# A DiT attention block with adaptive layer norm: V before Q and K, from the scale alone, and the shift's share of V added after P V

## The chip, the core and the metric

The kernel runs on one core of one Trainium2 chip. The metric is device time in microseconds (us) of one execution; lower is better. Five engines work side by side, each in the order of its own queue: TensorE (PE, with its weight loads PEld), VectorE (DVE), ScalarE (ACT), GpSimd (POOL) and SyncE (SP), which here only issues DMA transfers. PE writes to PSUM alone, which has eight banks; the other engines work on SBUF and PSUM (POOL here on SBUF alone).

## The reference

B = 2 samples of N = 256 tokens, D = 1152, all inputs bfloat16. `w_mod` is 1152 x 6912, `wqkv` 1152 x 3456, `wo` 1152 x 1152.

```python
mod = (_silu(c) @ w_mod).reshape(B, 6, 1, D)
shift_a, scale_a, gate_a, shift_m, scale_m, gate_m = [mod[:, i] for i in range(6)]
h = _layernorm(x, axis=-1) * (1 + scale_a) + shift_a
qkv = h @ wqkv
q, k, v = (qkv[..., :D].copy(), qkv[..., D:2 * D].copy(), qkv[..., 2 * D:].copy())
p = _softmax(jnp.einsum('bqd,bkd->bqk', q, k) * D ** (-0.5), axis=-1)
a = jnp.einsum('bqk,bkd->bqd', p, v) @ wo
return x + gate_a * a
```

Only the first three of the six parts of `mod` are used. The rows of `p` sum to 1, so a term of `v` that is the same for every token of a sample, such as `shift_a @ wv`, comes out of `p @ v` unchanged.

## The kernel before

The 512 tokens are four tiles of 128 (`TT`); the 1152 features are nine groups of 128 (`KT`). Everything fits in SBUF: 19.8 MB are read once.

*Start.* `c` and x tiles 0 and 2 come on SP's queue, x tiles 1 and 3 on ACT's. PE transposes `c`, then runs 13 matmuls of no use (`junk_ps`). `silu(c)` is laid out 96 times side by side (`scT_rep`, L173), so that the small products for scale and shift have 96 and 56 columns instead of 2. DVE makes the statistics and normalised tiles (`xn`) of tokens 0 to 2, ACT those of tile 3; the reciprocal root is made on POOL for tiles 0 to 2. PE transposes `xn` and DVE and ACT copy it to `xnT` (features on partitions).

*Scale.* `scale_block(kk)`: nine matmuls for each of nine row blocks `wm` of `w_mod`, which arrive in nine transfers (L146). A first matmul with a row of ones puts the 1 of 1 + scale into PSUM. Then DVE makes `hTs = xnT * (1 + scale)`, 18 pieces of 128x256.

*First five features of Q.* They are begun from `hTs`, before the shift is known: `qkv_step(k)` (L302) adds feature group k to five banks `accs`; the weights `wA` come in three transfers. Among these steps stand the shift's matmuls (`shift_block`, L309; `H_AFTER_K` says after which step). When the shift is there, its share of the five features is made by 45 matmuls of 2 columns (`bias_ps`, L329) and added when the banks are emptied to `qkT`; 18 pieces `hT = xnT * (1 + scale) + shift` are made on DVE (12) and ACT (6).

*The other 13 features of Q and K* are made from `hT`, one bank each, and copied by ACT (L383). Then the scores S (`s_ps`, L414), then V, twelve groups of 128x384 (`v_group`, L429), under which softmax runs on DVE and ACT. Then P is transposed, then P V for both samples (L485), copied to `attnT` two feature groups at a time, then the output projection with gate and residual, tile by tile (L498). The last 384 columns of the last tile use weights already multiplied by the gate (`wo_last`, nine products on POOL, L483).

*Gate.* `gacc` (L397): DVE multiplies nine row blocks of `w_mod`'s third part with `silu(c)` and adds them, for each sample; `partition_all_reduce` on POOL (L409) sums over partitions and broadcasts. The second all-reduce is tied behind the softmax by a dependency (L464).

*Order.* Part of each of PE's, DVE's and ACT's order is pinned by hand (`pe_seq`, `dve_seq`, `act_seq`, L533); the rest is set by the scheduler. PSUM is 5 banks `mm` and 3 `pre`. SP issues the weights in the order in which they are used; an issue waits until the eighth transfer before it has landed.

Of the kernel before, what the change touches and what calls it, by code (L numbers as in the profile page):

```python
# [16 lines left out]
def kernel(  # L17
# [8 lines left out]
):  # L26
    nc = tc.nc
    P = 128
    B, N, D = x.shape
    T = B * N  # L30
    KT = D // P
    TT = T // P
# [5 lines left out]

    NACC = 5
    WA = NACC * P  # L40
    KSPLIT = 4
    NRS = 96
    NRH = 56
    KH = (KT + 1) // 2
    H_AFTER_K = [4, 4, 4, 5, 5, 6, 6, 6, 6]
    N_JUNK = 13
# [4 lines left out]
    wmod_v = w_mod.rearrange("(kk p) (s n) -> p kk s n", p=P, s=6)  # L51

# [5 lines left out]
    psum = ctx.enter_context(tc.tile_pool(name="psum", bufs=5, space=PSUM))  # L58
    psum_pre = ctx.enter_context(tc.tile_pool(name="psum_pre", bufs=3, space=PSUM))

    SCHED = mybir.DependencyInfo(mybir.DependencyClass.NoSync, mybir.DependencyReason.SCHED_ONLY)
    pe_seq = []
    dve_seq = []
    act_seq = []

    class _Rec:

        def __init__(self, eng, seq):
            self._eng, self._seq = eng, seq
# [12 lines left out]
    vec = _Rec(nc.vector, dve_seq)  # L82
    sca = _Rec(nc.scalar, act_seq)
    ten = _Rec(nc.tensor, pe_seq)

    def pin(seq):
        names, insts = set(), []
        for r in seq:
            if r.ins.name not in names:
                names.add(r.ins.name)  # L90
                insts.append(r)
        for a, b in zip(insts, insts[1:]):
            tc.add_manual_dep(b.ins, a.ins.name, SCHED, reason="pinned engine order")

    ident = const.tile([P, P], BF16)
    nc.gpsimd.memset(ident, 0.0)
    nc.gpsimd.affine_select(
# [3 lines left out]
    ones_bf = const.tile([P, P], BF16)  # L101
    nc.gpsimd.memset(ones_bf, 1.0)
    ones_row = const.tile([1, 512], BF16)
    nc.gpsimd.memset(ones_row, 1.0)
    junk_rhs = const.tile([P, 512], BF16)
    nc.gpsimd.memset(junk_rhs, 1.0)
    eps_t = const.tile([P, 1], F32)
    nc.gpsimd.memset(eps_t, EPS)
    neg_half = const.tile([P, 1], F32)
    nc.gpsimd.memset(neg_half, -0.5)  # L110

    c_sb = const.tile([2 * KT, P], BF16)
    x_sb = act.tile([P, TT, D], BF16)
    nc.scalar.preload_act_table_set("natural_log_exp_and_others")
    nc.sync.dma_start(out=c_sb, in_=c.rearrange("b (k p) -> (b k) p", p=P))  # L115
    for t in range(TT):
        eng = nc.sync if t % 2 == 0 else nc.scalar
        eng.dma_start(out=x_sb[:, t, :], in_=x_f[t * P : (t + 1) * P, :])

    wA = wpool.tile([P, KT, WA], BF16)  # L120
    rest_chunks = [(WA, 2 * P), (WA + 2 * P, 3 * P)]
    c0 = WA + 5 * P
    while c0 < 2 * D:
        w_ = min(CW, 2 * D - c0)
        rest_chunks.append((c0, w_))
        c0 += w_
    for vc in range(NCH):
        rest_chunks.append((2 * D + vc * CW, CW))
    wq_rest = []
    for i, (c0, w_) in enumerate(rest_chunks):  # L130
        wq_t = wpool.tile([P, KT, w_], BF16, tag=f"wq_rest{i}")
        wq_rest.append(wq_t)

    def w_cols(col, width):
        if col + width <= WA:
            return wA, col
        for (c0, w_), t_ in zip(rest_chunks, wq_rest):
            if c0 <= col and col + width <= c0 + w_:
                return t_, col - c0
        raise AssertionError((col, width))  # L140

    wmpool = ctx.enter_context(tc.tile_pool(name="wmpool", bufs=1))
    wmS, wmH = [], []
    for kk in range(KT):
        wm = wmpool.tile([P, D], BF16, tag=f"wS{kk}")
        nc.sync.dma_start(out=wm, in_=wmod_v[:, kk, 1, :])  # L146
        wmS.append(wm)
    nc.sync.dma_start(out=wA[:, 0:1, :], in_=wqkv_v[:, 0:1, 0:WA])
    nc.sync.dma_start(out=wA[:, 1:KSPLIT, :], in_=wqkv_v[:, 1:KSPLIT, 0:WA])
    nc.sync.dma_start(out=wA[:, KSPLIT:, :], in_=wqkv_v[:, KSPLIT:, 0:WA])  # L150
    for kk in range(KT):
        wm = wmpool.tile([P, D], BF16, tag=f"wH{kk}")
        nc.sync.dma_start(out=wm, in_=wmod_v[:, kk, 0, :])
        wmH.append(wm)

    cT_ps = psum_pre.tile([P, 2 * KT], BF16, tag="pre")
    pe_seq.append(ten.transpose(cT_ps, c_sb, ident[: 2 * KT, : 2 * KT]))
    junk_ps = psum_pre.tile([P, 512], F32, tag="pre")
    for jj in range(N_JUNK):
        ten.matmul(junk_ps, lhsT=ident, rhs=junk_rhs, start=True, stop=True)  # L160
    e_sb = small.tile([P, 2 * KT], F32, tag="e_sb")
    act_seq.append(sca.activation(out=e_sb, in_=cT_ps, func=ACT.Exp, scale=-1.0))
    dve_seq.append(vec.tensor_scalar_add(out=e_sb, in0=e_sb, scalar1=1.0))
    dve_seq.append(vec.reciprocal(out=e_sb, in_=e_sb))
    scT_f = const.tile([P, KT, B], F32)
    dve_seq.append(vec.tensor_tensor(
        out=scT_f.rearrange("p k b -> p b k"),
        in0=cT_ps.rearrange("p (b k) -> p b k", b=B),
        in1=e_sb.rearrange("p (b k) -> p b k", b=B),
        op=ALU.mult,  # L170
    ))
    scT_rep = const.tile([P, KT, NRS // B, B], BF16)
    dve_seq.append(vec.tensor_copy(out=scT_rep, in_=scT_f.unsqueeze(2).to_broadcast([P, KT, NRS // B, B])))  # L173

    def sc_rhs(kk, n):
        return scT_rep[:, kk].rearrange("p r b -> p (r b)")[:, 0:n]

    mv_all = const.tile([P, TT, 2], F32)
    rstd = const.tile([P, TT], F32)
    nb = const.tile([P, TT], F32)  # L180
    xn = act.tile([P, TT, D], BF16, tag="a1")
    xnT = act.tile([P, KT, T], BF16, tag="a2")

    def dve_stats(t):
        stats = small.tile([P, NCH, 6], F32, tag="stats")
        for s in range(NCH):
            dve_seq.append(vec.bn_stats(out=stats[:, s, :], in_=x_sb[:, t, s * CW : (s + 1) * CW]))
        dve_seq.append(vec.bn_aggr(out=mv_all[:, t, :], in_=stats))
        nc.gpsimd.tensor_scalar_add(out=rstd[:, t : t + 1], in0=mv_all[:, t, 1:2], scalar1=EPS)
        nc.gpsimd.tensor_tensor(out=rstd[:, t : t + 1], in0=rstd[:, t : t + 1], in1=neg_half, op=ALU.pow)  # L190

    def dve_norm(t):
        dve_seq.append(vec.scalar_tensor_tensor(
            out=nb[:, t : t + 1], in0=mv_all[:, t, 0:1], scalar=-1.0, in1=rstd[:, t : t + 1],
            op0=ALU.mult, op1=ALU.mult,
        ))
        dve_seq.append(vec.tensor_scalar(
            out=xn[:, t, :], in0=x_sb[:, t, :], scalar1=rstd[:, t : t + 1], scalar2=nb[:, t : t + 1],
            op0=ALU.mult, op1=ALU.add,
        ))  # L200

    def act_stats_norm(t):
        ssum = small.tile([P, 1], F32, tag="ssum")
        act_seq.append(sca.activation(out=xn[:, t, :], in_=x_sb[:, t, :], func=ACT.Copy, accum_out=ssum))
        nmean = small.tile([P, 1], F32, tag="nmean")
        act_seq.append(sca.activation(out=nmean, in_=ssum, func=ACT.Copy, scale=-1.0 / D))
        ssq = small.tile([P, 1], F32, tag="ssq")
# [8 lines left out]
    def evac(idx, out_ap, in_ap):  # L216
        if idx % 2 == 0:
            return vec.tensor_copy(out=out_ap, in_=in_ap)
        return sca.copy(out=out_ap, in_=in_ap)
# [346 lines left out]
```

## Time and profile before

| what | value |
|---|---|
| median of 3 runs | 103.38 us (103.31 to 103.44) |
| span of the profiled execution | 101.7 us (101.74) |
| PE busy | 93.7 us, 723 matmuls |
| DVE busy | 71.9 us |
| ACT busy | 30.4 us |
| POOL busy | 28.5 us |
| read from HBM | 19.76 MB |

The page cuts the span in 40 slices of 2.54 us; a digit is the busy share of an engine in tenths. The chain of waits goes from the last instruction back to what released each one. In the timeline a line is: start, duration (us), engine, line, operation, output <- inputs, count, and in brackets the engine's idle time before it. Nearly all instructions carry the line of the recording helper (L75), so they are told apart by the names of their tiles. A matmul's own duration is longer than the distance to the next one; what counts in a sum is the distance.

### The profile page before, as it was taken

How to read it: one execution, taken by the hardware profiler on the slowest of the kernel's cores; microseconds unless marked ns; L12 is line 12 of the kernel's file. 1: busy time of each engine (PE TensorE's matmuls, PEld its weight loads, DVE VectorE, ACT ScalarE, POOL GpSimd, SP SyncE). 2: the span in 40 equal slices, each digit the busy share in tenths (PEclk: the TensorE clock that was granted, in tenths of full speed). 3: DMA queues.
4: the chain of work that ended last, by engine and by line, in shares of the span. 5: the costliest groups of instructions: out<-in, count | busy, mean ns of one | idle time of the engine just before them, and what ended most of it. 6: DMA issues, size and time to landing. Idle time of an engine off the chain costs nothing.

```text
span 101.7 us, 1828 instructions
## 1 busy us (share of the span) xinstructions
PE 93.7 (92%) x723; PEld 55.8 (55%) x729; DVE 71.9 (71%) x129; ACT 30.4 (30%) x61; POOL 28.5 (28%) x28
## 2 busy tenths in 40 slices
PE   0996989997999999999999999999998999999970
PEld 0334974474564444444447866566567856566550
DVE  0999679200899999999999992155226859998760
ACT  5089560000678422422332013551115500000000
POOL 6033300000000000079910000007990039996000
PEclk9999999999999999999999999999999999999999
DMA  2989999999999999999999100000000000202212
GB/s 75 376 304 396 403 391 386 405 395 325 354 374 361 400 377 322 316 327 327 368 406 366 50 0 0 0 0 0 0 0 0 6 0 0 116 0 116 114 54 67
DMA packets 17204, 21.05 MB, mean 207 GB/s; under 512 B 1068, under 2 KB 11692, under 8 KB 17196
## 3 DMA queue, kind: packets, MB, share of 16 engines
q1 hardware_dynamic: 16763, 20.34, 57.3%
q10 hardware_dynamic: 432, 0.61, 1.8%
q8 instruction: 5, 0.08, 0.3%
q14 instruction: 4, 0.02, 0.1%
HBM read 19.76 MB, written 1.18 MB: 206 GB/s over the span
## 4 chain that ended last, share of the span: by engine, by line
PE 71%; DMA 24%; issue 1%; DVE 0%; SPq 0%; ACT 0%
PE ps L75 63%; DMA wm<-in_w_mod_dram 21%; PE s_ps L75 4%; DMA x_sb<-in_x_dram 3%; PE acc_t L75 2%; PE bias_ps L75 1%; DVE pT L75 0%; PE psH L75 0%; SPq L115 0%; PE pT_ps L75 0%; ACT o_sb L75 0%
## 5 line engine op out<-in xcount | busy, mean ns | idle before, releaser
L409 POOL PARTITION_ALL_REDUCE gate_bc<-gacc x2 | 14.1, 7068 | 50.8 <-DVE gacc L75 32.9
L75 DVE SCALAR_TENSOR_TENSOR gacc<-wg_t,scT_f,gacc 128x1152 f32<-128x1152 bf16 x16 | 27.4, 1714 | 0.6
L75 PE MATMUL ps<-hT,wq_t 128*128 128x512 bf16 x114 | 25.3, 379 | 0.2
L75 PEld LDWEIGHTS <-wq_t 128*128 128x128 bf16 x117 | 11.3, 98 | 13.6
L75 PE MATMUL ps<-wq_t,hT 128*128 128x384 bf16 x108 | 17.7, 326 | 0.0
L75 PE MATMUL ps<-wo_t,attnT 128*128 128x384 bf16 x99 | 16.3, 326 | 0.0
L75 PEld LDWEIGHTS <-attnT 128*128 128x128 bf16 x117 | 10.9, 98 | 6.7
L75 PEld LDWEIGHTS <-hT 128*128 128x128 bf16 x108 | 10.6, 98 | 6.9
L75 ACT CAST qkT<-ps 128x512 bf16<-128x512 f32 x13 | 7.6, 585 | 15.4 <-PE ps L75 15.4
L483 POOL TENSOR_TENSOR wo_last<-wo_t,gate_bc 128x384 bf16<-128x384 bf16 x9 | 9.9, 1136 | 7.1 <-issue 7.1
L75 PE MATMUL acc_t<-hTs,wA 128*128 128x512 bf16 x42 | 9.9, 379 | 0.5 <-DVE hTs L75 0.4
L75 DVE TENSOR_TENSOR o_sb<-ga,x_sb 128x384 bf16<-128x384 f32 x11 | 8.1, 736 | 0.4
L75 PEld LDWEIGHTS <-wA 128*128 128x128 bf16 x90 | 5.4, 96 | 5.1 <-issue 0.5
L75 PEld LDWEIGHTS <-wm 128*128 128x128 bf16 x162 | 6.4, 97 | 3.1 <-DMA wm<-in_w_mod_dram 2.3
L75 ACT CAST v_sb<-ps 128x384 bf16<-128x384 f32 x8 | 3.8, 478 | 14.0 <-PE ps L75 14.0
L75 DVE TENSOR_TENSOR ga<-ps,gate_bc 128x384 f32<-128x384 f32 x11 | 6.1, 553 | 2.6 <-PE ps L75 2.5
L75 ACT ACTIVATE hT<-xnT,sh,s1p 128x256 bf16<-128x256 bf16 x6 | 3.1, 588 | 11.7 <-DVE sh L75 11.7
L75 PE MATMUL mps<-scT_rep,wm 128*128 128x96 bf16 x81 | 4.8, 207 | 0.8 <-DMA wm<-in_w_mod_dram 0.7
L75 DVE CAST sh_bf<-psH 128x18 bf16<-128x18 f32 x1 | 0.2, 176 | 7.4 <-PE psH L75 7.4
L75 ACT CAST o_sb<-ps 128x64 bf16<-128x64 f32 x1 | 0.2, 212 | 17.4 <-PE ps L75 17.4
L75 PE MATMUL junk_ps<-junk_rhs,ident 128*128 128x512 bf16 x13 | 4.6, 528 | 0.3 <-POOL neg_half L110 0.3
L75 DVE CAST v_sb<-ps 128x384 bf16<-128x384 f32 x4 | 2.1, 553 | 3.8 <-PE ps L75 3.8
(70 smaller groups left out, 81.3 us busy)
## 6 DMA issues: line engine op xcount, KB each, us to landing
wm<-in_w_mod_dram SPq DMA_DIRECT2D x18, 288.0 KB, 6.6
wq_t<-in_wqkv_dram SPq DMA_DIRECT2D x6, 864.0 KB, 9.7
wg_t<-in_w_mod_dram SPq DMA_DIRECT2D x9, 288.0 KB, 7.1
wo_t<-in_wo_dram SPq DMA_DIRECT2D x9, 288.0 KB, 6.2
wq_t<-in_wqkv_dram SPq DMA_DIRECT2D x2, 576.0 KB, 9.2
out_dram<-o_sb SPq DMA_DIRECT2D x3, 288.0 KB, 2.1
wA<-in_wqkv_dram SPq DMA_DIRECT2D x1, 800.0 KB
x_sb<-in_x_dram ACTq DMA_DIRECT2D x2, 288.0 KB, 3.5
```

Source lines behind the costliest of these rows:

```text
L75: r = fn(*a, **k)
L409: ar = nc.gpsimd.partition_all_reduce(gate_bc[:, b, :], gacc[:, b, :], P, bass.bass_isa.ReduceOp.add)
L483: nc.gpsimd.tensor_tensor(out=wo_last[:, k, :], in0=wo_k[k][:, D - TAILW :], in1=gate_bc[:, B - 1, D - TAILW :], op=ALU.mult)
```

## The change

V is made first, before the shift is known and before Q and K. It is made from `hTs` alone, and the shift's share of V, `shift @ wv` (`bias_ps`, now 81 matmuls of 2 columns, on PE after S), is added when P V is emptied to `attnT` (`bv`), one feature group at a time.

- The scale comes in two parts, four feature groups (`wS0`) and five (`wS1`), each three transfers of three row blocks, and two groups of matmuls. The right side has 2 columns (`scT`); `scT_rep` is gone.
- V's first 768 columns are begun by token tile, for the first four feature groups (`v_mm(t, range(K0))`), as soon as `wS0` and `wvA`'s first parts are there. They need two banks for each sample's two tiles plus one shared one (`vps`). The `hTs` pieces of these four groups are 128x128 and read the transposes straight from PSUM (`hts_early`, DVE); the other groups' transposes are copied to `xnT` by ACT (`evac_late`). The ninth group's transposes of all four tiles share a bank (`tp8`).
- Then come the second part of the scale, the other five groups of `hTs`, the other steps of V, and V's last 384 columns (`v_last`) with the shift's matmuls (`shift_group`) between them. Then `hT = hTs + shift`, and all 18 features of Q and K from `hT`, each copied by ACT.
- P V of sample 0 and output tiles 0 and 1 come before P V of sample 1; softmax of sample 1 stands on DVE between `pT` of sample 0 and the `attnT` pieces of sample 0.
- The tie of the second all-reduce behind the softmax is gone; all of POOL's and SP's order is pinned too.
- x comes on SP alone, `c` on ACT; 8 useless matmuls instead of 13; tokens 2 and 3 take their statistics on ACT, 0 and 1 on DVE; the products with which a tile is normalised are all on DVE. `wo` comes in three transfers, the gate's rows in two.
- PSUM is 7 banks `mm` and 1 `pre`. In the built program the 7 go round like this: the useless matmuls, transposes of tile 0, `tp8`, transposes of tile 1, `vps` (three) of sample 0; then transposes of tile 2 take the first one, the `vps` of tile 2 those of tiles 0's and 1's transposes (after `evac_late` of these), transposes of tile 3 those of tile 2, and `vps` of tile 3 that of tile 3's transposes (after `evac_late(3)`). `evac_late(t)` waits for all four pieces of `hts_early(t)`, which read the same bank.

The diff, cut (removed lines are in the listing above):

```diff
-    NACC = 5
-    WA = NACC * P
-    KSPLIT = 4
-    NRS = 96
-    NRH = 56
-    KH = (KT + 1) // 2
-    H_AFTER_K = [4, 4, 4, 5, 5, 6, 6, 6, 6]
-    N_JUNK = 13
+    K0 = 4
+    VA = 768
+    N_JUNK = 8
...
+    psum = ctx.enter_context(tc.tile_pool(name="psum", bufs=7, space=PSUM))
+    psum_pre = ctx.enter_context(tc.tile_pool(name="psum_pre", bufs=1, space=PSUM))
...
+    sca.dma_start(out=c_sb, in_=c.rearrange("b (k p) -> (b k) p", p=P))
     nc.scalar.preload_act_table_set("natural_log_exp_and_others")
...
     for t in range(TT):
...
+        sp.dma_start(out=x_sb[:, t, :], in_=x_f[tcol(t), :])
+    K1 = KT - K0
+    wS0 = wpool.tile([P, KT, K0 * P], BF16, tag="wS0")
+    wS1 = wpool.tile([P, KT, K1 * P], BF16, tag="wS1")
+    wvA = wpool.tile([P, KT, VA], BF16)
+    wvB = wpool.tile([P, KT, D - VA], BF16)
+    for g in range(3):
+        ks = slice(3 * g, 3 * g + 3)
+        sp.dma_start(out=wS0[:, ks, :], in_=wmod_v[:, ks, 1, 0 : K0 * P])
+    for ks in (slice(0, 2), slice(2, K0)):
+        sp.dma_start(out=wvA[:, ks, :], in_=wqkv_v[:, ks, 2 * D : 2 * D + VA])
+    for g in range(3):
+        ks = slice(3 * g, 3 * g + 3)
+        sp.dma_start(out=wS1[:, ks, :], in_=wmod_v[:, ks, 1, K0 * P : D])
+    for ks in (slice(K0, K0 + 2), slice(K0 + 2, KT)):
+        sp.dma_start(out=wvA[:, ks, :], in_=wqkv_v[:, ks, 2 * D : 2 * D + VA])
+    sp.dma_start(out=wvB, in_=wqkv_v[:, :, 2 * D + VA : 3 * D])
+    wH = []
+    for g in range(3):
+        wh = wpool.tile([P, 3, D], BF16, tag=f"wH{g}")
+        sp.dma_start(out=wh, in_=wmod_v[:, 3 * g : 3 * g + 3, 0, :])
+        wH.append(wh)
...
+    pool.tensor_tensor(
         out=scT_f.rearrange("p k b -> p b k"),
...
+        in0=cT_sb.rearrange("p (b k) -> p b k", b=B),
         in1=e_sb.rearrange("p (b k) -> p b k", b=B),
         op=ALU.mult,
...
+    )
+    pool.tensor_copy(out=scT, in_=scT_f)
...
+    def norm_act(t):
+        vec.tensor_scalar(out=xn[:, t, :], in0=x_sb[:, t, :], scalar1=nmean[:, t : t + 1],
+                          scalar2=rstd[:, t : t + 1], op0=ALU.add, op1=ALU.mult)
...
+        tp = psum.tile([P, KT - 1, P], BF16, tag="mm")
+        tps[t] = tp
+        if not tp8:
+            t8 = psum.tile([P, TT, P], BF16, tag="mm")
+            tp8.append(t8)
+        for k in range(KT - 1):
+            ten.transpose(tp[:, k, :], xn[:, t, k * P : (k + 1) * P], ident)
+        ten.transpose(tp8[0][:, t, :], xn[:, t, (KT - 1) * P :], ident)
...
+    psS0 = psum_pre.tile([P, K0, B], F32, tag="pre")
+    def scale_block(ps, wt, n, kk):
+        if kk == 0:
+            ten.matmul(ps.rearrange("p j b -> p (j b)"), lhsT=ones_row, rhs=ones_row[:, 0 : n * B],
+                       start=True, stop=False, skip_group_check=True)
+        for j in range(n):
+            ten.matmul(ps[:, j, :], lhsT=wt[:, kk, j * P : (j + 1) * P], rhs=scT[:, kk, :],
+                       start=False, stop=(kk == KT - 1), skip_group_check=True)
+    def hts_early(t):
+        b = t // NQ
+        for k in range(K0):
+            vec.tensor_scalar(out=hTs[:, k, tcol(t)], in0=tps[t][:, k, :], scalar1=psS0[:, k, b : b + 1],
+                              scalar2=None, op0=ALU.mult)
+    def evac_late(t, eng):
+        (eng.copy if eng is sca else eng.tensor_copy)(out=xnT[:, 0 : K1 - 1, tcol(t)], in_=tps[t][:, K0 : KT - 1, :])
+    vps = {}
+    def v_mm(t, ks):
+        b, i = divmod(t, NQ)
+        if (b, 2) not in vps:
+            vc_t = psum.tile([P, NQ, VA - 512], F32, tag="mm")
+            vps[b, 2] = vc_t
+        if (b, i) not in vps:
+            va_t = psum.tile([P, 512], F32, tag="mm")
+            vps[b, i] = va_t
+        for k in ks:
+            lhsT = hTs[:, k, tcol(t)]
+            ten.matmul(vps[b, i], lhsT=lhsT, rhs=wvA[:, k, 0:512], start=(k == 0), stop=(k == KT - 1))
+            ten.matmul(vps[b, 2][:, i, :], lhsT=lhsT, rhs=wvA[:, k, 512:VA], start=(k == 0 and i == 0),
+                       stop=(k == KT - 1), skip_group_check=True)
+    for s in range(NCH):
+        bn(0, s)
+    aggr(0)
+    bn(1, 0)
+    bn(1, 1)
+    norm_bn(0)
+    bn(1, 2)
+    aggr(1)
+    act_sum(2)
+    act_ssq(2)
+    act_sum(3)
+    act_ssq(3)
+    norm_bn(1)
+    transposes(0)
+    for kk in range(KT):
+        scale_block(psS0, wS0, K0, kk)
+    transposes(1)
+    hts_early(0)
+    hts_early(1)
+    v_mm(0, range(K0))
+    norm_act(2)
+    evac_late(0, sca)
+    evac_late(1, sca)
+    v_mm(1, range(2))
+    transposes(2)
+    v_mm(1, range(2, K0))
+    hts_early(2)
+    evac_late(2, sca)
+    norm_act(3)
+    v_mm(2, range(2))
+    transposes(3)
+    v_mm(2, range(2, K0))
+    hts_early(3)
+    evac_late(3, sca)
+    sca.copy(out=xnT[:, K1 - 1, :], in_=tp8[0].rearrange("p t q -> p (t q)"))
+    v_mm(3, range(K0))
+    psS1 = psum_pre.tile([P, K1, B], F32, tag="pre")
+    for kk in range(KT):
+        scale_block(psS1, wS1, K1, kk)
+    for k in range(K0, KT):
+        for b in range(B):
+            vec.tensor_scalar(out=hTs[:, k, bcol(b)], in0=xnT[:, k - K0, bcol(b)],
+                              scalar1=psS1[:, k - K0, b : b + 1], scalar2=None, op0=ALU.mult)
+    for k in range(K0, KT - 2):
+        for t in range(TT):
+            v_mm(t, (k,))
+    v_sb = act.tile([P, TT, D], BF16, tag="a1")
+    for b in range(B):
+        for i in range(NQ):
+            v_mm(b * NQ + i, (KT - 2,))
+        for i in range(NQ):
+            v_mm(b * NQ + i, (KT - 1,))
+        sca.copy(out=v_sb[:, b * NQ, 0:512], in_=vps[b, 0])
+        vec.tensor_copy(out=v_sb[:, b * NQ + 1, 0:512], in_=vps[b, 1])
+        sca.copy(out=v_sb[:, b * NQ : (b + 1) * NQ, 512:VA], in_=vps[b, 2])
...
+    psH = psum_pre.tile([P, KT, B], F32, tag="pre")
+    def shift_group(g):
+        for kk in range(3 * g, 3 * g + 3):
+            for j in range(KT):
+                ten.matmul(psH[:, j, :], lhsT=wH[g][:, kk - 3 * g, j * P : (j + 1) * P], rhs=scT[:, kk, :],
+                           start=(kk == 0 and j == 0), stop=(kk == KT - 1), skip_group_check=True)
+    def v_last(t, eng):
+        ps = psum.tile([P, D - VA], F32, tag="mm")
+        for k in range(KT):
+            ten.matmul(ps, lhsT=hTs[:, k, tcol(t)], rhs=wvB[:, k, :], start=(k == 0), stop=(k == KT - 1))
+        (eng.copy if eng is sca else eng.tensor_copy)(out=v_sb[:, t, VA:D], in_=ps)
+    v_last(0, vec)
+    shift_group(0)
+    v_last(1, sca)
+    shift_group(1)
+    v_last(2, vec)
+    shift_group(2)
...
+    vec.tensor_copy(out=sh, in_=psH)
...
+                sca.activation(out=hT[:, k, bcol(b)], in_=hTs[:, k, bcol(b)], func=ACT.Identity,
+                               bias=sh[:, k, b : b + 1], scale=1.0)
             else:
...
+                vec.tensor_scalar(out=hT[:, k, bcol(b)], in0=hTs[:, k, bcol(b)], scalar1=sh[:, k, b : b + 1],
+                                  scalar2=None, op0=ALU.add)
+    vec.tensor_copy(out=sh_bf, in_=sh)
+    v_last(3, sca)
...
+        wq_t = wpool.tile([P, KT, CW], BF16, tag=f"wqk{i}")
...
+    for i in range(2):
+        sp.dma_start(out=wqk[i], in_=wqkv_v[:, :, i * CW : (i + 1) * CW])
+    wgA = wpool.tile([P, K0, D], BF16, tag="wS0")
+    sp.dma_start(out=wgA, in_=wmod_v[:, 0:K0, 2, :])
+    sp.dma_start(out=wqk[2], in_=wqkv_v[:, :, 2 * CW : 3 * CW])
+    wgB = wpool.tile([P, K1, D], BF16, tag="wS1")
+    sp.dma_start(out=wgB, in_=wmod_v[:, K0:KT, 2, :])
+    for i in range(3, 2 * NCH):
+        sp.dma_start(out=wqk[i], in_=wqkv_v[:, :, i * CW : (i + 1) * CW])
+    wo_g = []
+    for g in range(3):
+        wo_t = wpool.tile([P, 3, D], BF16, tag=f"wH{g}")
+        sp.dma_start(out=wo_t, in_=wo_v[:, 3 * g : 3 * g + 3, :])
+        wo_g.append(wo_t)
...
+    for f in range(2 * KT):
+        ps = psum.tile([P, T], F32, tag="mm")
         for k in range(KT):
...
+            ten.matmul(ps, lhsT=wqk[f // NF][:, k, (f % NF) * P : (f % NF + 1) * P], rhs=hT[:, k, :],
+                       start=(k == 0), stop=(k == KT - 1))
+        sca.copy(out=qkT[:, f, :], in_=ps)
...
+        for kt in range(KT):
+            wg = wgA[:, kt, :] if kt < K0 else wgB[:, kt - K0, :]
+            if kt == 0:
+                vec.tensor_scalar(out=gacc[:, b, :], in0=wg, scalar1=scT_f[:, 0, b : b + 1], scalar2=None,
+                                  op0=ALU.mult)
+            else:
+                vec.scalar_tensor_tensor(out=gacc[:, b, :], in0=wg, scalar=scT_f[:, kt, b : b + 1],
+                                         in1=gacc[:, b, :], op0=ALU.mult, op1=ALU.add)
+        pool.partition_all_reduce(gate_bc[:, b, :], gacc[:, b, :], P, bass.bass_isa.ReduceOp.add)
...
+    bias_ps = psum_pre.tile([P, KT, B], F32, tag="pre")
+    for j in range(KT):
         for k in range(KT):
...
+            wt = wvA[:, k, j * P : (j + 1) * P] if j * P < VA else wvB[:, k, j * P - VA : (j + 1) * P - VA]
+            ten.matmul(bias_ps[:, j, :], lhsT=wt, rhs=sh_bf[:, k, :], start=(k == 0), stop=(k == KT - 1))
+    bv = const.tile([P, KT, B], F32)
...
+            for dd in range(ndv):
+                dv = dv0 + dd
+                if gi % 2 == 0:
+                    vec.tensor_scalar(out=attnT[:, dv, bcol(b)], in0=ps[:, dd, :], scalar1=bv[:, dv, b : b + 1],
+                                      scalar2=None, op0=ALU.add)
+                else:
+                    sca.activation(out=attnT[:, dv, bcol(b)], in_=ps[:, dd, :], func=ACT.Identity,
+                                   bias=bv[:, dv, b : b + 1], scale=1.0)
...
-    SYNC_SCHED = mybir.DependencyInfo(mybir.DependencyClass.Sync, mybir.DependencyReason.SCHED_ONLY)
-    tc.add_manual_dep(gate_ars[B - 1].ins, dve_seq[-1].ins.name, SYNC_SCHED, reason="keep gpsimd off the shared port")
...
+    softmax(0)
+    vec.tensor_copy(out=bv, in_=bias_ps)
+    p_transposes(0)
+    softmax(1)
+    pv(0)
+    for k in range(KT):
+        pool.tensor_tensor(out=wo_last[:, k, :], in0=wo_k(k, slice(D - TAILW, D)),
+                           in1=gate_bc[:, B - 1, D - TAILW :], op=ALU.mult)
+    out_tile(0)
+    p_transposes(1)
+    out_tile(1)
+    pv(1)
+    out_tile(2)
+    out_tile(3)
+    for r in (ten, vec, sca, pool, sp):
+        r.pin()
```

## The prediction

> **What bounds the kernel now.** I read the page first, then the chain of waits, then the timeline. The profiled execution has a span of 101.74 us, and the times have a median of 103.38, so 1.64 us lie around the span.
>
> ```profile
> PE 93.7 (92%) x723; PEld 55.8 (55%) x729; DVE 71.9 (71%) x129; ACT 30.4 (30%) x61; POOL 28.5 (28%) x28
> ...
> PE   0996989997999999999999999999998999999970
> ...
> GB/s 75 376 304 396 403 391 386 405 395 325 354 374 361 400 377 322 316 327 327 368 406 366 50 0 0 0 0 0 0 0 0 6 0 0 116 0 116 114 54 67
> ```
>
> PE is busy nearly everywhere. Transfers matter up to slice 10.
>
> ```profile
> 4.39 6.42 DMA wm<-in_w_mod_dram
> ...
> 19.56 5.82 DMA wm<-in_w_mod_dram
> ...
> 31.33 10.74 PE ps L75 x49
> ...
> 54.37 3.93 PE s_ps L75 x36
> 58.30 17.55 PE ps L75 x108
> 75.85 0.24 PE pT_ps L75 x4
> 76.09 0.02 issue
> 76.11 0.43 DVE pT L75
> 76.55 0.05 issue
> 76.59 21.86 PE ps L75 x155
> ```
>
> The chain names transfers up to 25.38 us and PE from there to 98.45. But the timeline shows that PE has little room before 25 us either:
>
> ```profile
> 14.52 3.69 DVE L75 TENSOR_SCALAR hTs<-xnT,mps 128x256 bf16<-128x256 bf16 x18
> ...
> 15.16 5.55 PE L75 MATMUL acc_t<-hTs,wA 128*128 128x512 bf16 x24 [0.41 <-DVE hTs L75]
> ...
> 27.83 1.27 PE L75 MATMUL bias_ps<-sh_bf,wA 128*128 128x2 bf16 x45
> ```
>
> From 15.16 us on PE runs dense: nine `acc_t` steps of 5 (45 x 0.216 = 9.7), shift 2.6, bias 1.3, 13 features 25.4, S 3.9, V 17.6 sum to 60.5, and 15.16 + 60.5 = 75.7 is where V ends. So the bound is PE's work from the first real matmul on, and a reordering pays only by an earlier start or fewer waits.
>
> **Prices.** A 512-column matmul costs 10.74/49 = 0.219 us, a 256-column one 3.93/36 = 0.109, a 384-column one 17.55/108 = 0.1625, a 2-column one 1.27/45 = 0.028.
>
> **The earlier start.** `wm` number 5 brings the bytes to nine transfers of 0.295 MB (2.65 MB) and lands at 4.39 + 6.42 = 10.81; SP's issues that wait for such landings come 0.72 apart (8.62, 9.35, 10.11, 10.83), so 2.36 MB are in at 10.1. The change needs just that (x and the first 4 columns of the scale, `wS0`) before the first `hTs`. Its rows are 1 KB instead of 2.3 KB: between no loss and the pace of the slices with 768-byte rows (320 against 400 GB/s, 0.7 us for 1.18 MB); I take 0.35. Landed 10.45, last 12 scale matmuls 0.35, then `wvA`'s first part, 0.39 MB or 1.0 us behind `wS0`: V starts at 11.5 instead of `acc_t` at 15.16, a gain of 3.7. Lower bound: by the page's slices 2.36 MB have moved at 8.7 us already, 1.4 before that landing. c and x change queues; SP issues its four x and three `wS0` transfers at 0.43 each by 3.7 us, while x itself keeps the link filled, so that is free. 8 junk matmuls for 13, and no widened `scT_rep` (1.05 us of DVE at 3.32), lie under the same transfers: nothing, as do the two small products on POOL that now make `scT` (needed when `wS0` lands). Gone are ten biased `qkT` outputs (2.05 us on DVE, 2.04 on ACT); ScalarE copies all 18 features instead, 0.58 each under 1.95 of PE.
>
> **PE's work from there.** Early V 16 x (0.219 + 0.109) = 5.25; transposes of tiles 2 and 3 1.1 (0.55 each, nine in about that at 10.54 and 13.31); second scale group 45 x 0.028 = 1.27; late V 20 x 0.328 = 6.56; last columns of V 36 x 0.1625 = 5.85; shift 81 x 0.028 = 2.29; Q and K 18 x 1.95 = 35.1 (13 took 25.4); S 3.93; bias of V 2.29. Together 63.6, against 60.5 before: the bias grew by 1.0, and transposes and scale now stand behind the start. 11.5 + 63.6 = 75.1. So 0.6 is left of the 3.7, before waits. The matmuls with 2 columns might cost the 0.032 of the 56-column ones (27 in 0.86): +1.0 for all 243.
>
> **New waits before Q and K.** PE's order is fixed, so a matmul that waits holds everything behind it.
> - `wvA` part 2 lands 1.0 after part 1, PE has 0.66 of work: 0.4.
> - `hts_early(t)`: four 128x128 products out of PSUM. Not in the trace; the 256-wide ones from SBUF come 0.205 apart, a PSUM copy of 512 takes 0.42. I take 0.2 (0.1 and 0.42 are the ends). `norm_act(3)` (0.58, as `xn`) stands behind the four of tile 2 on DVE, and transposes(3) behind it: after tile 2's transposes at 14.4, 0.15 + 0.85 + 0.6 = 16.0; PE has 1.3 of V in hand to 15.7. 0.4.
> - v_mm(3) takes the PSUM bank that transposes(3) filled, and ScalarE's copy out of it comes after DVE's four: 16.6 + 0.15 + 0.85 + 0.6 (ACT copies 512 in 0.58) = 18.2 against 17.2. 1.0.
> - The first late `hTs` after the second scale group: 0.5 (0.41 before, 256 wide as then).
> - Shift ends, `sh` 0.17, six ScalarE products (0.5 apart, 3.06 for 6): the ninth step of the first feature starts 3.4 behind; last V tile (1.46) and eight steps cover 3.0. 0.4.
>
> Sum 2.7, if the 0.42 held 2 more, if 0.1, 0.8 less. Bias of V ends at 77.8. The weights are no wait: shift's last part is 9.14 MB, 1.18 more than at 25.38, so by 29; PE asks at 34. wqk's six tiles follow in PE's order and land 5 us or more ahead of it.
>
> **The tail.** P^T to P V 0.74 as at 75.85. Before, both P V stood together and softmax lay under V. Now softmax(1) (reduce, exp, scaling: 66.35 to 69.06, 2.71) sits on DVE between pT(0) and the outputs of P V(0). These are five of 0.395 on DVE (`qkT` with its bias: five in 2.05), the last at 2.71 + 1.97 = 4.7; PE has 1.97 of P V and 1.3 of the chunk's first eight steps. A wait of 1.5. For out_tile(2) the same five stand behind one output chunk (0.56 + 0.69): 0.2. Second P^T: 0.25. So 21.86 + 1.95 = 23.8. 77.8 + 0.74 + 23.8 = 102.4; to the end 3.29 as before; around it 1.64: **107.3 us**.
>
> **Gate.** The change drops the dependency that kept the second all-reduce behind softmax.
>
> ```profile
> 43.99 7.30 POOL L409 PARTITION_ALL_REDUCE gate_bc<-gacc  x1 [32.88 <-DVE gacc L75]
> ...
> L75 DVE SCALAR_TENSOR_TENSOR gacc<-wg_t,scT_f,gacc x16: 1417/1419/6143, 32.3 to 59.5; 128x1152 f32<-128x1152 bf16 x16
> ```
>
> Inside the first all-reduce one of 16 accumulations takes 6.14 instead of 1.42: it ends at 50.76, so DVE was held until 49.3, 5.35 after the all-reduce began. In the change gacc starts behind ScalarE's `hT` (38.2); `wgB` (14.45 MB in, at some 355 GB/s from 7.96 MB at 25.4) lands at 43.5; five accumulations to 50.8; the second half takes 17.2 as from 43.75 to 60.94, so 68.0; all-reduce to 74.9, DVE held until 68.0 + 5.35 = 73.4. S(0) is ready at 73.6 and its maximum at 74.5. A cost of nothing, with 0.9 us of cover: had S come earlier, the chain 73.4 + 2.1 (softmax from `nmx` on) = 75.5 would be the floor for P^T. wo_last follows 7.1 after (as before), 82 to 92, needed at 100.
>
> The Trainium skill's SBUF — State Buffer (Who interferes with whom) has a rule against this edit: VectorE's two-port modes are shut out for a whole GpSimd instruction, single-input ops included. The rows show it only for the two-input accumulation; by the rule `nmx` is held too, at the times above still for nothing.
>
> **Rivals.**
> 1. *PE's clock drops again.* Junk matmuls come 0.43 apart until 5.57, then four in 0.74. Between 6 and 11 us the change gives PE some 2 us of work instead of nearly 5. If the slow pace returns, the first 3.3 us of V (junk needed as long, 2.63 to 5.98) take twice the time: +1.6 net, 108.9. Against: no gap is longer than 1.4. TensorE: Matmul & The Clock Gate (HAM oscillation — how this bites in real kernels) asks only that no idle gap exceeds about 3.4 us; by it nothing is lost and the time is 107.3. Chance 0.2.
> 2. *Not slower: evacuations hide.* Place: the five waits before Q and K and the one before out_tile(0). If DVE and ScalarE deliver before PE asks (products at 0.1, copies overlapping), 2.7 + 1.5 go; P^T is then at the gate's floor of 75.5: 75.5 + 0.74 + 22.3 + 4.9 = 103.4, and 0.3 less if `wgB` lands that much earlier: 103.1. It decides when PE's waits after 11.5 sum to under 0.5. For: they are sums of pipelined steps; against: each names a fixed order. Chance 0.15.
> 3. *Gate chain late.* `wgB` 2 us later (its five transfers in front share the 320 GB/s pace) and `nmx` held: 75.4 instead of 74.5, 108.2. Chance 0.1.
>
> **Numbers.** Forecast 0.55, by itself 105.3 to 108.3 (start 1.4 earlier; the 0.42 partly). The 8-in-10 range is 104.4 to 109.6: it takes in rivals 1 and 3 and half the way to 2. Under 0.2% can't be told from no change. Faster 0.12 and same 0.03 are rival 2; slower 0.85 is the rest.
>
> **What would show it.** V's first matmul at 11.5; PE idle about 1 us before the fourth tile's V, for an ACT copy; Q and K from 36 to 71.6; bias of V 2.3 behind S; 1.5 us of PE idle for DVE's `attnT` before the first output. Wrong if V starts after 13 or before 10, if these waits are missing, or if softmax(0) waits for an all-reduce.

## The result: 6% slower, with PE's clock halved for 6.8 us at V's start

After: 109.51 us (median of 4 runs, 108.07 to 109.66), beside 103.34 (103.21 to 103.44) for the kernel before on the same chip: ratio 1.0572, 95% interval 1.0511 to 1.0633. Slower had been forecast, and 109.5 is just inside the stated range of 104.4 to 109.6; the predicted time, 107.3, was 2.2 too low. The profiled execution took 109.39 with a span of 107.6. Ratios, here and below, leave out executions more than 1.5% above the fastest of the same kernel.

The page of the kernel after, its busy times, its rows for PE and its clock, and two groups:

```profile
PE 95.4 (89%) x759; PEld 55.6 (52%) x759; DVE 68.3 (63%) x124; ACT 31.3 (29%) x65; POOL 27.9 (26%) x28
...
PE   0953899689999999999999999999987899999980
...
PEclk9998558999999999999999999999999999999999
...
L73 PE MATMUL ps<-wo_t,attnT 128*128 128x384 bf16 x99 | 17.1, 327 | 1.1 <-DVE attnT L73 1.0
...
L73 PE MATMUL va_t<-wvA,hTs 128*128 128x512 bf16 x36 | 13.8, 422 | 1.4 <-ACT xnT L73 0.9
```

PE gained 1.7 us of busy time and the span 5.9. The clock row has a dip in slices 4 to 7, from 10.15 to 16.98 us: just where V begins. Before the change it was

```profile
PEclk9999999999999999999999999999999999999999
```

The last column of the two groups above shows two of the waits that were forecast. The same stretch by windows (length, PE busy, granted clock, DMA share, GB/s):

```profile
6.74:10.15 3.41, 1.33 (x26) 1.00 1.05 350
10.15:13.56 3.41, 2.77 (x37) 0.50 1.06 377
13.56:16.98 3.42, 3.42 (x17) 0.50 1.07 367
16.98:20.39 3.41, 2.90 (x26) 1.00 1.08 350
```

And PE's timeline there (start, duration, instruction, count, idle time before it):

```profile
8.58 0.45 PE L73 MATMUL psS<-scT,wS 128*128 128x2 bf16 x12 [0.66 <-DMA wS<-in_w_mod_dram]
10.06 0.47 PE L73 MATMUL psS<-scT,wS 128*128 128x2 bf16 x12 [1.02 <-DMA wS<-in_w_mod_dram]
11.16 0.48 PE L73 MATMUL psS<-scT,wS 128*128 128x2 bf16 x12 [0.64 <-DMA wS<-in_w_mod_dram]
11.50 1.01 PE L73 MATMUL tp<-ident,xn 128*128 128x128 bf16 x8
...
12.42 0.63 PE L73 MATMUL va_t<-wvA,hTs 128*128 128x512 bf16 x1
...
13.06 0.63 PE L73 MATMUL va_t<-wvA,hTs 128*128 128x512 bf16 x1
...
17.11 0.38 PE L73 MATMUL va_t<-wvA,hTs 128*128 128x512 bf16 x1
...
17.43 0.38 PE L73 MATMUL va_t<-wvA,hTs 128*128 128x512 bf16 x1
...
21.10 0.38 PE L73 MATMUL va_t<-wvA,hTs 128*128 128x512 bf16 x1 [0.94 <-ACT xnT L73]
```

V starts at 12.42. Its pairs (512 and 256 columns) come 0.64 apart up to 16.3 and 0.33 apart from 17.11 on: six pairs at half speed cost 6 x 0.31 = 1.9, and the next tile's transposes (0.85 from 16.26 to 17.11, against 0.50 from 18.86 to 19.36) some 0.3. At 21.10 is the forecast wait for ScalarE's copy. The tail, in the timeline of all engines:

```profile
80.43 0.68 DVE L73 TENSOR_REDUCE mx<-s_ps 128x2 f32<-128x512 f32 x1
80.56 2.12 PE L73 MATMUL ps<-pT,v_sb 128*128 128x256 bf16 x18 [0.52 <-DVE pT L73]
...
82.66 0.62 DVE L73 TENSOR_SCALAR pn<-p_f,rinv 128x256 bf16<-128x256 f32 x2
83.19 1.26 DVE L73 TENSOR_SCALAR attnT<-ps,bv 128x256 bf16<-128x256 f32 x3
...
83.73 0.89 PE L73 MATMUL ps<-wo_t,attnT 128*128 128x384 bf16 x3 [1.04 <-DVE attnT L73]
```

softmax(1) keeps VectorE from 80.43 to 83.2, the copies of P V(0)'s outputs to `attnT` come behind it, and PE stands idle for 1.04.

PE's way to its end, as the prediction had it and as it came:

| us | predicted | after |
|---|---|---|
| V's first matmul | 11.5 | 12.42 |
| PE busy from there | 86.0 | 88.69, of it 2.2 for the low clock |
| PE idle from there | 4.9 | 3.29 |
| PE's end | 102.4 | 104.40 |
| to the end, and around the span | 3.29 + 1.64 | 3.2 + 1.8 |

(Predicted idle: 2.7 before Q and K, 1.7 in the tail, 0.5 for P^T; busy is what is left of 102.4 - 11.5.)

### The profile page after: what moved, and what is told of

It reads as the page before. It is cut to its first block, busy times and chain, and to the rows that moved or that the text cites. A ratio compares the mean times of both kernels' runs of the same rounds, so it can differ in the third digit from the quotient of the medians.

```text
span 107.6 us, 1856 instructions
## 1 busy us (share of the span) xinstructions
PE 95.4 (89%) x759; PEld 55.6 (52%) x759; DVE 68.3 (63%) x124; ACT 31.3 (29%) x65; POOL 27.9 (26%) x28
## 4 chain that ended last, share of the span: by engine, by line
PE 79%; DMA 7%; DVE 4%; SPq 2%; ACT 2%; issue 1%; ACTq 0%; DVEq 0%
PE ps L73 57%; PE va_t L73 7%; DMA wS<-in_w_mod_dram 7%; PE s_ps L73 4%; PE vc_t L73 4%; SPq L73 2%; PE tp L73 2%; PE bias_ps L73 2%; PE psH L73 2%; DVE hTs L73 2%; PE psS L73 2%; ACT xnT L73 1%; ACT p_f L73 1%; DVE attnT L73 1%; DVE pn L73 1%
## 5 line engine op out<-in xcount | busy, mean ns | idle before, releaser
L73 PE MATMUL ps<-hT,wq_t 128*128 128x512 bf16 x162 | 35.1, 379 | 0.0
L73 PEld LDWEIGHTS <-wq_t 128*128 128x128 bf16 x162 | 15.9, 98 | 19.0
L73 PEld LDWEIGHTS <-hTs 128*128 128x128 bf16 x108 | 10.8, 103 | 8.8 <-issue 1.7
L73 PE MATMUL va_t<-wvA,hTs 128*128 128x512 bf16 x36 | 13.8, 422 | 1.4 <-ACT xnT L73 0.9
L73 DVE SCALAR_TENSOR_TENSOR gacc<-wgB,scT_f,gacc 128x1152 f32<-128x1152 bf16 x10 | 14.2, 1419 | 0.4
L73 DVE SCALAR_TENSOR_TENSOR gacc<-wgA,scT_f,gacc 128x1152 f32<-128x1152 bf16 x6 | 13.2, 2206 | 0.2
L73 PE MATMUL vc_t<-wvA,hTs 128*128 128x256 bf16 x36 | 10.7, 297 | 0.0
L73 DVE TENSOR_SCALAR hTs<-tp,psS 128x128 bf16<-128x128 bf16 x16 | 3.5, 282 | 6.5 <-PE tp L73 4.2
L73 PE MATMUL ps<-wvB,hTs 128*128 128x384 bf16 x36 | 6.5, 325 | 0.0
L73 PE MATMUL ps<-pT,v_sb 128*128 128x256 bf16 x36 | 4.3, 272 | 0.5 <-DVE pT L73 0.5
## 6 DMA issues: line engine op xcount, KB each, us to landing
wh<-in_w_mod_dram SPq DMA_DIRECT2D x3, 864.0 KB, 11.1
```

The lines of the kernel that those rows point to most:

```text
L73: r = fn(*a, **k)
```

## The experiments

The theory to be tested: what the forecast's sum lacked is the prediction's rival 1, PE's clock, and the rest is waits as predicted. Against it stand two rivals: transfers and waits alone set the time; the clock depends on gaps in PE's work. Times are medians; each stands beside runs of the kernel before on its chip (103.1 to 103.4).

### Junk that keeps the clock

```diff
     for kk in range(KT):
+        if kk % 3 == 0:
+            for _ in range((3, 4, 2)[kk // 3]):
+                ten.matmul(junk_ps, lhsT=ident, rhs=junk_rhs, start=True, stop=True)
         scale_block(psS0, wS0, K0, kk)
```

> Nine more 512-column junk matmuls where PE waits for the first scale columns (3, 4 and 2 ahead of the three transfers' groups). Theory (the clock of PE fell for want of work, rival 1 of the prediction): the clock stays full from about 6 us on, V's pairs of matmuls come 0.33 apart from the first, and the time falls by some 1.9 (six pairs at 0.64, the transposes at 0.9 to 1.0), to 107.6. Rival (the waits for weights and evacuations set the pace, the low clock only fills them): the clock is full and the time falls by under 0.6, to 109 or more. Second rival (the clock falls whatever PE does): the clock is low at 10 us again, time 109.5.

107.91, ratio 1.0479 (1.0416 to 1.0542): the theory. The clock row has no dip any more, and in the timeline V's first pairs stand 0.32 apart:

```profile
PEclk9999999999999999999999999999999999999997
```

```profile
12.51 0.38 PE L73 MATMUL va_t<-wvA,hTs 128*128 128x512 bf16 x1
...
12.83 0.38 PE L73 MATMUL va_t<-wvA,hTs 128*128 128x512 bf16 x1
...
13.57 0.38 PE L73 MATMUL va_t<-wvA,hTs 128*128 128x512 bf16 x1 [0.26 <-DMA wvA<-in_wqkv_dram]
```

The third line shows the forecast wait for `wvA` part 2, which the slow clock had covered. Adding 1.9 us of useless work made the kernel faster by 1.6 (medians) or 1.0 (0.93% between the ratios, each known to 0.6%).

The same edit with narrow junk:

```diff
-            for _ in range((3, 4, 2)[kk // 3]):
-                ten.matmul(junk_ps, lhsT=ident, rhs=junk_rhs, ...)
+            for _ in range((26, 35, 17)[kk // 3]):
+                ten.matmul(junk_ps[:, 0:2], lhsT=ident, rhs=junk_rhs[:, 0:2], ...)
```

> As e1_junk, but its 9 junk matmuls of 512 columns between the scale groups are replaced by 78 of 2 columns, which keep PE busy for about the same time (78 x 0.025 = 1.95 us against 9 x 0.213 = 1.92). Theory (columns streamed in a stretch of 3.41 us decide: in the traces so far all 36 stretches with under 3,150 of at most 8,192 were followed by half the clock, all 356 with over 3,180 by the full one): the stretch behind the junk has some 1,300 columns, the clock falls near 10 us for two stretches, 109.4. Rival (time that PE is busy, or the gaps, decide): clock full, 107.9 as e1_junk.

109.01, ratio 1.0568 (1.0506 to 1.0631): the theory by its time. The two profiled executions differ by 1.1, and that lies ahead of P^T(0), which starts at 79.06 here and at 77.93 in e1_junk; a dip of the clock from 80.28 to 83.69 comes behind it. The window with the narrow junk, and V's matmuls in the timeline:

```profile
8.60:12.01 3.41, 3.12 (x105) 1.00 1.03 354
```

```profile
12.72 0.63 PE L73 MATMUL va_t<-wvA,hTs 128*128 128x512 bf16 x1
...
15.68 0.38 PE L73 MATMUL va_t<-wvA,hTs 128*128 128x512 bf16 x1
```

PE was busy for 3.12 of 3.41 us there (2.90 of 3.40 in e1_junk), and yet V ran at half speed. The 1.00 in the clock's column means nothing here: this trace's first clock record is at 15.42, the view fills in 1.00 before it, and the durations tell the pace. So in this execution the clock did not fall, as was expected, but was never raised before 15.42, whereas e1_junk's was full from its first record at 6.08. The pair shows that 3.12 us of busy time in 3.41 do not raise the clock; what makes it fall is answered by all traces together, below. The eight junk matmuls at the start, 3.4 us at half speed, do not always raise it: e3_scale2_first's profile shows the slow pace too, with its first clock record at 17.94.

With the five junk matmuls that the change had taken away:

```diff
-    N_JUNK = 8
+    N_JUNK = 13
```

> The change with 13 junk matmuls ahead instead of 8, as before. Theory (columns in each stretch decide): the junk fills the stretch to about 9.5 us, the next has under 1.1 us of columns up to V's start, so the clock falls one stretch later, near 13, for 3.4 us or more: 109.0 to 109.8. Rival (five junk matmuls were all that was missing): clock full, 107.7 as e1_junk.

108.00 (1.041 to 1.0561). By the time this is nearer to the rival, but the clock was not full, so the five junk matmuls were not all that was missing:

```profile
PEclk9998599999999999999999999999985999999999
```

The theory in turn missed the place and the time: the clock was low from 9.87 to 13.28, of which 1.97 us lie behind V's start at 11.31, and again in the tail, from 78.14 to 81.55. V began 1.1 earlier than in the change, since the last of `wS0` had landed at 10.01 instead of 11.12; why it landed earlier isn't shown.

The kernel before with narrow scale matmuls and 8 junk ones, all else kept:

```diff
-    N_JUNK = 13
+    N_JUNK = 8
-        mps = psum_pre.tile([P, KH, NRS], F32, tag="pre")
+        mps = psum_pre.tile([P, KH, B], F32, tag="pre")
-                rhs=sc_rhs(kk, NRS),
+                rhs=sc_rhs(kk, B),
```

> The kernel before, with two of the change's cuts alone: scale matmuls of 2 columns instead of 96, 8 junk matmuls instead of 13. All order and transfers as before. Theory (the clock falls when few columns stream in a stretch of 3.4 us): a low clock is on record somewhere between 8 and 17 us, and the time rises by what of it lies behind 15.2 (0.3 to 2.2): 103.5 to 105.5. Rival (only a gap of over about 3.4 us drops it, as the Trainium skill's TensorE: Matmul & The Clock Gate says in HAM oscillation; PE's gaps here stay under 1.5): full clock, the time within 0.2 of before.

1.005 of before (1.0023 to 1.0078), the lower end of what the theory allowed. That ratio goes by five of ten executions: three of 103.5 to 103.6 with a mean granted clock of 0.99 or more, and two of 103.9 and 104.0 with 0.96. The other five took 105.1 to 107.0, three of them with a clock of 0.95 and two with 0.99 or more, so the price of the low clock can't be read from this kernel's times. The clock row of the profiled execution, 105.13, shows the fall itself:

```profile
PEclk9997555799999999999999999999999999999999
```

The clock is low from 9.16 to 19.40, with no gap of PE over 1.3 us in the stretch before. The Trainium skill's TensorE: Matmul & The Clock Gate (HAM oscillation) asks only that no idle gap exceeds about 3.4 us; here that was kept and the clock fell all the same, so the measurement decides. The edit takes away two things at once, and neither was taken away alone; in the kernel before, the stretches of 3.41 us from 5.96, 9.37 and 12.78 have some 5,200, 6,570 and 6,560 columns, and 1,820, 3,460 and 2,590 of these belong to the wide scale matmuls.

### Order of the copies, of x, and of softmax

```diff
-    v_mm(3, range(K0))
     psS1 = ...
     for kk in range(KT):
         scale_block(psS1, wS1, K1, kk)
+    v_mm(3, range(K0))
```

> The second scale group (46 matmuls, 1.2 us) goes ahead of the fourth tile's early V on PE. Theory (PE's 0.94 us of waiting for ScalarE's copy of tile 4, and the 0.46 for the first late hTs, are order, with the scale group at hand to fill the first and to make the second early): 1.3 less, 108.2. Rival (the evacuations are too slow whatever the order, the wait comes back at the late V): under 0.4 less, 109.1 or more.

108.51 (1.0461 to 1.058). From V's first matmul to the first late one it took 10.64 (12.86 to 23.50) instead of 11.92 (12.42 to 24.34), with the low clock over the same six pairs: 1.28 gained, as the theory had it. The clock of this execution was low from 79.38 to 82.79 as well, which that of the change was not; that this gave back part of the gain is likely and not shown.

```diff
-        sp.dma_start(out=x_sb[:, t, :], ...)
+        (sp if t % 2 == 0 else sca).dma_start(out=x_sb[:, t, :], ...)
```

> Tiles 1 and 3 of x are issued by ScalarE's queue again, as before the change. The prediction's assumption (SP's seven issues in a row are hidden under the transfers): nothing, 109.5 within 0.3. Rival (the single queue makes x and the first scale columns late: 7.41 and 11.12 against the 10.45 that was predicted): the last of them lands by 10.6, V starts 0.5 earlier, 109.0 or less.

108.84 (1.0482 to 1.0623): not told apart from the change. In the profile the rival's signs are there: the last of `wS0` landed at 10.51 and V began at 11.81, 0.6 earlier; but that execution took 109.40, as long as the change's. Over all traces with four feature groups in the early part it lands at 11.1 to 11.6 with one queue in five of six (10.0 in j1_junk13), and at 10.2 to 11.2 with two queues in five; so two queues look earlier, but the scatter is as wide, and the cause isn't shown.

```diff
-    softmax(1)
     pv(0)
+    softmax(1)
```

> On VectorE and ScalarE softmax(1) stands behind the outputs of P V(0) instead of ahead of them; PE's order is kept. Theory (the 1.04 us of idle PE ahead of the first output are softmax(1) on VectorE): that idle time is gone and the time falls by 1.0, to 108.5. Rival (the wait moves on: P^T(1) or the gated outputs now wait for softmax(1)): under 0.3 less, 109.2 or more.

110.34 (1.062 to 1.0755): slower than both. The first output waits for nothing any more, but the clock row of this run shows why that is no reading of the order: in a second dip, 81.33 to 84.74, P V(0) took 3.19 instead of 2.12.

```profile
PEclk9997559999999999999999999999995899999999
```

So the edit was repeated on a version whose start (its head, up to V) keeps the clock. That version alone has the edits of e3_scale2_first and e4_x_two_queues and

```diff
-    N_JUNK = 8
+    N_JUNK = 12
     for kk in range(KT):
         scale_block(psS0, wS0, K0, kk)
-    transposes(1)
+        if kk == 5:
+            transposes(1)
+        for _ in range({2: 3, 5: 2}.get(kk, 0)):
+            ten.matmul(junk_ps, lhsT=ident, rhs=junk_rhs, start=True, stop=True)
```

> The three cures of the head together: 12 junk matmuls ahead and 5 among the scale groups, transposes(1) ahead of the third group, x on two queues, the second scale group ahead of the fourth tile's early V. The rest as in the change. S(0) then ends some 1.9 earlier than in e1_junk, at 72. Theory (the gate is the floor: e1_junk's nmx took 1.16 instead of 0.17 and ended with the second all-reduce, at 76.0): nmx waits for the all-reduce's end near 75.5, P^T(0) starts near 77.5 as in e1_junk, and the time is 107.3 to 107.9. Rival (the all-reduce holds nothing that matters): P^T(0) at 76, time 106.0.

106.47 (1.0275 to 1.0354), between the two and nearer to the rival. S(0)'s maximum came 1.56 earlier than in e1_junk, `nmx` was held only until 74.2, 5.1 after the all-reduce began, and the scaling of P ended with the bias, at 76.3: PE did not wait for the gate. With softmax(1) moved behind P V(0) as well:

> h1_head (clock held) with the edit of e2_softmax_after_pv: softmax(1) behind the outputs of P V(0) on VectorE and ScalarE. Theory (the idle PE ahead of the first output, 1.37 in h1_head, is softmax(1) on VectorE; e2_softmax_after_pv was slower for its clock alone): 105.3. Rival (the wait only moves to P^T(1) and the outputs): 106.2 or more.

108.31 (1.0434 to 1.0533): the theory fell. The 1.37 us ahead of the first output are gone, but 1.28 came back ahead of the third tile's output, as the rival had it, and in this execution the all-reduce of the gate did count. Its timeline:

```profile
69.30 6.83 POOL L73 PARTITION_ALL_REDUCE gate_bc<-gacc  x1 [9.75 <-DVE gacc L73]
...
72.20 2.23 DVE L73 TENSOR_SCALAR nmx<-mx 128x2 f32<-128x2 f32 x1
...
76.33 0.65 PE L73 MATMUL pT_ps<-ident,pn 128*128 128x128 bf16 x4 [0.92 <-DVE pn L73]
```

A product of two numbers per partition, 0.17 elsewhere, took 2.23, ending 5.13 after the all-reduce began, and P^T was 0.92 late; then the clock was at half from 76.16 to 82.99, and P V(0) took 4.00 instead of 2.12. All four executions had a mean granted clock of 0.967 to 0.984, where three of h1_head's four had 1.0. So this pair does not price the order with the clock held either; it shows that the wait moves on.

### All mended

The next edit mends the gate, the bias and the tail as well. Its core, on h1_head (`softmax_a` is softmax up to the exponentials, `softmax_b` the scaling; `pv` takes its groups as a list; `wgA` and `wgB` are issued behind the first and the second `wqk`; v_last(2) stands where v_last(3) stood):

```diff
-    gacc = act.tile([P, B, D], F32, tag="a3")
+    gacc = act.tile([P, B, D], F32, tag="a2")
         sca.copy(out=qkT[:, f, :], in_=ps)
+        if 5 <= f < 17 and f % 2 == 1:
+            bias_block((f - 5) // 2)
...
+    softmax_a(0)
+    softmax_b(0)
+    softmax_a(1)
+    v_last(3, sca)
+    p_transposes(0)
+    for j in (6, 7, 8):
+        bias_block(j)
+    softmax_b(1)
+    vec.tensor_copy(out=bv, in_=bias_ps)
+    pv(0, (0, 1, 2))
+    p_transposes(1)
+    pv(0, (3, 4))
+    pv(1, range(5))
...
+    for t in range(TT):
+        out_tile(t)
```

> h1_head, and behind it: the gate's weights one and two transfers earlier and its sums in the buffer of xnT; 54 of the 81 matmuls of the bias spread over Q and K, 27 behind P^T(0); the last columns of V's fourth tile behind S; both P V ahead of the outputs, softmax(1) ahead of P V(0)'s outputs on VectorE only. Theory (with the clock, the gate and the order mended, PE's work alone is left): second all-reduce ends near 73.3, P^T(0) at 75.3, to PE's end 22.5, to the end 3.3, around it 1.6: 102.7, below before. Rival (the change's PE work, more by 3.1 than before's, eats it): 104 or more.

105.58 (1.0188 to 1.0274). QK, S and P^T(0) came as expected (75.0), the tail did not: PE stood 1.27 for P^T(1)'s copy, behind four `attnT` on DVE. With another order there (P^T(0) copied by ScalarE):

```diff
     softmax_a(0)
-    softmax_b(0)
     softmax_a(1)
+    softmax_b(0)
+    softmax_b(1)
...
-    pv(0, (0, 1, 2))
     p_transposes(1)
-    pv(0, (3, 4))
+    pv(0, range(5))
     pv(1, range(5))
```

> h2_gate_early with another order behind S: both maxima and exponentials ahead of both scalings, P^T(0) copied by ScalarE, P^T(1) ahead of P V(0). Theory (h2_gate_early's missing 2.9 are idle PE behind P^T(0): 0.18, 0.23, 1.27, and the late start of the outputs, all of it DVE's order): outputs start at 80.3 instead of 82.5, 103.3. Rival (DVE is simply full there): under 0.7 less, 104.9 or more.

Ratio 1.004 (1.0009 to 1.0072), 103.9: the order was the cause. The ratio goes by the three executions of 103.6 to 104.1; the profiled one took 105.72, with the clock low from 9.63 to 13.04 and V only from 13.87. But in its tail, from P^T(0) to PE's end, it took 23.78 instead of 25.43, 1.65 less. With a smaller early part (the gate's weights change buffers with it):

```diff
-    K0 = 4
+    K0 = 3
```

> h3_tail_order with 3 instead of 4 columns of blocks (K0) in the early part: 0.29 MB less of the scale and 0.2 MB less of V ahead of PE's start; the gate's weights in other buffers, in the same order of use. Theory (the head of PE is set by bytes, 0.58 and 0.21 of waiting for V's weights in h2_gate_early): V starts 0.8 earlier, 102.6. Rival (what is taken from the early part comes back as waits for the second scale group or the copies of P^T's... tile 3 and 4): 103.3 or more.

Ratio 1.0025 (0.9995 to 1.0055), 103.6 beside 103.39: the same as before. This goes by the two executions of 103.55 and 103.70; the other two took 105.3 with a mean granted clock of 0.983, so half of them still lost the clock for a while. V starts only 0.4 earlier than in h2_gate_early, since DVE's `hTs` now come last (0.39). No version beat the kernel before. PE's window from its first V matmul to its end in h4_k3, and from the first `acc_t` in the kernel before:

```profile
11.18:98.60 87.42, 86.01 (x698) 1.00 0.59 202
```

```profile
15.16:98.45 83.29, 82.15 (x589) 1.00 0.55 190
```

V starts 4.0 us earlier than `acc_t` did, and behind it are 3.9 more work and 0.3 more idle time: the earlier start was given back in full. Before, transposes and scale matmuls lay ahead of the start, under transfers, and the bias was 45 matmuls instead of 81.

### The gate on the clock

All 14 traces together, worked out from them: the clock changes only at multiples of 3.413 us from its first record. Count the columns that matmuls stream in each such stretch (a matmul's columns are spread from its start at the pace of the clock; 8,192 when PE runs dense, 16 x 512). Behind 409 stretches the clock is on record. It is half behind 24 of them, which have at most 3,057 columns, and full behind the other 385, which have at least 3,152. Ahead of a trace's first clock record only the pace of the matmuls tells the clock; there one stretch of 3,178 (e3_scale2_first) was still followed by the slow pace, so the limit is known to about 100 columns.

PE's busy time does not sort the stretches. In e3_scale2_first's from 75.97 PE was busy for 3.24 of 3.41 us with 2,574 columns, and half the clock followed; in h2_gate_early's from 77.99 it was busy for 2.03 with 3,975 columns, and the full clock followed. Transposes count like other matmuls: without them the two groups overlap. Some of the stretches:

| kernel, stretch from | columns | clock behind it |
|---|---|---|
| after, 6.74 | 1,190 | half |
| after, 10.15 (at half) | 2,569 | half |
| after, 13.56 (at half) | 4,096 | full |
| e1_junk, 6.08 | 3,321 | full |
| e2_softmax_after_pv, 77.91 | 2,713 | half |
| e1_junk, 74.35 | 3,749 | full |
| h5_head_softmax, 72.74 | 1,320 | half |

A scale, shift or bias matmul of 2 columns takes 0.025 us of PE and adds only 2 columns. Where the stretches begin differs from run to run, so one kernel can lose a stretch or not: with the 81 bias matmuls in one block behind S, five of nine profiled executions fell in the tail, that of the change not. Why the change's run of 108.07 was faster stays open: there is no trace of it, and its mean granted clock, 0.965, is no higher than the 0.968 of the other three.

## Why the prediction was right and wrong

- *The likeliest case assumed a full clock; rival 1, given 0.2, is what happened.* The step that failed is "8 junk matmuls for 13, and no widened `scT_rep` ... lie under the same transfers: nothing". The junk and the widened matmuls were what kept the clock: with both away it was at half from 10.15 to 16.98, with columns put back (e1_junk) it was full. With the five junk matmuls alone put back (j1_junk13) it still fell. The argument against the rival, "no gap is longer than 1.4", was true (the longest was 1.02) and beside the point. The rival's price was 1.6; e1_junk got 1.0 to 1.6 back, and the pairs and transposes in the trace lost 2.2. That 109.5 lies within the range is due to the range, which took this rival in, and not to the sum. With the clock held the sum fits better: e1_junk took 107.9, with PE's end at 102.95 against the 102.4 of the sum, though by errors of opposite sign.
- *Start, 11.5, came at 12.42.* Two terms of the sum: `wS0` landed at 11.12 instead of 10.45, and transposes(1), which stand on PE behind the whole scale group, were left out (0.92 at half clock, 0.55 at full). With them ahead of the last group and that landed at 10.27 (h2_gate_early) V waited for its weights alone, to 11.59.
- *PE's work, 86.0, was nearly right*: 88.69 less 2.2 is 86.5. The 2-column matmuls cost 0.025 instead of 0.028. (Of the 243 that the prediction counts for its +1.0, 36 lie ahead of V's start; behind it are 207, or 0.8.)
- *Waits, 4.9, were 3.3.* Right: v_mm(3) 0.94 for 1.0, late `hTs` 0.46 for 0.5, P^T 0.52. Right in size only: transposes(3) 0.28 for 0.4, since what came last there was ScalarE's copy (done at 18.80) and not the product on VectorE (18.62). Too large: out_tile(0) 1.04 for 1.5. Predicted, but not in the trace: `wvA` part 2 (0.4; covered by the slow clock, 0.26 in e1_junk), `hT` (0.4), out_tile(2) (0.2). So the two errors had opposite signs and part of the clock's price was hidden.
- *Gate at no cost: right.* The second all-reduce ended at 76.78, `nmx` took 0.22 instead of 0.17, and P was scaled at 78.8, before the bias ended at 79.8. Single-input operations were held too, as the rule that was cited said, but to 5.1 or 6.9 us from the start of an all-reduce recorded at 6.83, so not always for the whole of it; with an earlier S (h5_head_softmax) that cost 0.92.
- *Rival 2 (not slower)* fell with the waits; the mended kernels show that with the clock kept and most waits gone the change is a draw, not a gain.

## What to carry over

Price an earlier start against the work that it pulls out from under the transfers: here 4.0 us earlier met 3.9 us more on the path. A junk or widened matmul that looks like waste may be what holds TensorE's clock: before it is taken away, count streamed columns for each 3.4 us, as these traces ask, and not gaps or busy time. Compare kernels whose clock can fall only by traces with their clock rows beside them.

## What was not expected of the hardware

The sharp limit, between 3,057 and 3,178 of 8,192 columns in 3.413 us (some 38%), for falling and for rising alike. And the all-reduce seems to hold VectorE in two pieces: an `nmx` that began 2.9 or 4.2 us after its start was released at 5.13 (h1_head, h5_head_softmax), one that began 5.5 to 6.6 us after it at 6.86 (eight kernels, the change among them), whatever `nmx` itself needs (0.17).
